# Cosine attention and a gated MLP on one core: filler products on TensorE, one more turn by DMA, another order

## The chip, the core and the metric

The kernel runs on one core of a Trainium2 chip. The core has five engines with queues of their own: TensorE (PE, matrix products, with a separate queue entry for each load of a stationary operand, PEld), VectorE (DVE), ScalarE (ACT), GpSimd (POOL) and SyncE (SP, which here only issues DMAs). PE writes to PSUM, which DVE and ACT read; POOL works on SBUF alone. Sixteen DMA engines carry all transfers.

The metric is the device time of one execution in microseconds (us). Runs of one kernel differ a little, so the median of several is given.

## The reference

Attention on normalised q and k, for 8 batches of 12 heads, 448 positions, 64 elements a head; its output, 3584 tokens of 768, goes through two products with a gate between them.

```python
q_n = q / (np.linalg.norm(q, axis=-1, keepdims=True) + 1e-06)
k_n = k / (np.linalg.norm(k, axis=-1, keepdims=True) + 1e-06)
scores = np.matmul(q_n, k_n.transpose(0, 1, 3, 2)) / tau
attn = softmax(scores)                      # written out in the reference
x = (attn @ v).transpose(0, 2, 1, 3).reshape(3584, 768)
h = x @ w_in                                # 768 x 2048
out = (h / (1 + np.exp(-1.702 * h))) @ w_out  # 2048 x 768
```

## The kernel before

**Tiling.** The work is cut into 24 groups of four heads, numbered y = 0 to 23, three to a batch. Inputs are fp32, products fp16 with fp32 sums. For each group: q and k are loaded (lines 260 to 276), squared on ACT, POOL or DVE (298), summed on DVE (307), and the reciprocal norms are made (323 to 376: on ACT and DVE for the first batch, by a Newton iteration on DVE later). `scale` (399) multiplies q and k by them into `qks`. Then the heads' positions must go from partitions to columns. There are two ways. For y < TURNED PE does it: `turn_qk` (424) is seven 128x128 products with the identity matrix into a PSUM tile, and `turned_qk` (434) copies that tile to `qkT` on DVE or ACT; this is done once for k and once for q. For the other groups `dma_turn` (442) issues two DMA transposes from `qks` to `qkT` on SP. `last_keys` (452) copies the last 64 keys into a matrix of their own.

Scores (461 to 497) go to tiles `sp`, of which there are two; ACT makes the exponentials (499 to 520); `attend` (522) multiplies them with v, eight products of 65 or 130 columns for each half, with a column of ones that gives the row sums; `normalise` (548) divides on DVE; the result `xs` is turned again, on PE (574, 583) or by DMA (609), to `xT`. The first batch is cut in two halves of the query positions so that its results come sooner.

The MLP follows: `mm1` or `mm1_h` (618, 647) with w_in, tanh on ACT (629), `gate` on DVE (635, 659), `mm2` (672) with w_out in parts of four products, `halve` (684) on ACT or DVE, and stores on SP. PSUM has four tiles `mm` for turns, attention and MLP, besides the two of `sp`.

**Order.** The kernel fixes the order of all instructions itself. A planner (class `Plan`, 61 to 183) holds every step with its engine, an estimated duration, a due time, the steps that it follows and the buffers that it takes and frees. `order` (102) plays them through in planned time: at each moment each engine takes, of its ready steps with free buffers, the one with the earliest due time. `emit` (85) then writes the instructions in that order; on each engine they run strictly in it. Due times are shifted by one character each of the string `DUES`; where a step may run on several engines, the string `ENGINES` chooses. Transfers are modelled by a rate per packet and a fixed latency `DMA_US`. PE's durations in the plan are of its full clock (seven turns 0.45 us, a half-attend pair 0.5).

Some loads are held back: w_in until v of y = 1 has landed, w_out until q of y = 5 has, and the loads of y = 6 and later until w_out has (`HOLD`, 730).

The lines that the change touches most:

```python
TURNED = 2 * ND                                        # line 717; ND is 3
if y < TURNED: ...                                     # 792: turns of q and k on PE, else dma_turn
turned = y < TURNED                                    # 841: turns of the attention output on PE
if y >= TURNED: ...                                    # 855: else dma_turn_x
```

Of the kernel before, what the change touches and what calls it, by code (L numbers as in the profile page):

```python
# [21 lines left out]
SWITCH_US = 0.093  # L22
DMA_US = 1.9
START_US = 0.74
DMA_ENGINES = 16
PACKET_US = {256: 0.033, 1024: 0.072, 1536: 0.064, 1792: 0.078, 3072: 0.135, 4096: 0.178}
MOE_FROM, MOE_LAG = 8, 9
STEPS = "#$%&()*+,-./0123456789:;<=>?@ABCDEFGHIJKLMNOPQRSTUVWXYZ[]^_abcdefghijklmnopqrst"
DUES = (
    "LKQtTEKJLtIKrKKQKKK#K?MC[YRQPIKPKKK:LC3KFMKWKXgB/VK7K;eC]KKIKLWAH@@KMEKFKTTKCLKKmFBCKHQK=P>RD4S5TlMK1VkI"  # L30
    "IEPLYK:U[K9VUPKJPNLK:tKKKJAKKgKSG?LJKKXWINKJOKkKGWXZXLrK9UKKLVKJKFM#K<qK[SVK#WFKDPOLLKctlKKJQIILeZHWJJ9Q"
    "bJKKKKM@KWKK5RKKLKIWH:IGh^BXKP?U5AJK1LFKtAJtc^UcKWKt@JM^MfKJdKeKKRMZKL9UK9qrMgGdrXKcALc__8iHLdtntKctNt@M"
    "qBMtEKeRtKtQYjj3[CVKMetIJSRKIKP0KOK<AY9Ns1PsTXWLJcHtRjO;[BKO*(J#KFPkLtKKhgrLKttKSKcSIKK?KKLKFtKKN0##KMPA"
    "tLK_LGKHXQCKKOG_[LT];KMISK<RMmK8KcAJ(=UKAPJgNLHqELEKZpKKIs<KaDKjfKdKWJ5K4LKKaLK2KILLJEJK;JKgKKKZRK=KESIJ"
    "#?XF[HLKK#RBgWCZMYWRKKIHK2K,S3,QPQ?OKFI8aQE<BG:M@?MHVUJPLKQEt>UZNSKJGi$B#EJRKR=LLLJF:JKG@OK_MUKZKEKS#G>W"
    "VK]H_J*+tU7OSKDMGhLGZKSV@IKI]DK4K3>KLSCt#Kb#KdKgtDIFIQNLJI&URUVlKKGNDULN&PTK#L>CPESGQOKKOJKKKRRDKKKsj330"
    "##KM8LOK^G0#YQWt>GI@KLKeKUOHGKKKEKMPK&BV#><d6feK(#KD5HRNKBQTXs:YgZKKK36Kb<?CTKjH5#P1%KIQCKBND>LXQOTaQKKQ"
    "IKWn/HKOSRQLKBKIS<KKNKMLRFJNFJKNXKXMDQ_j-AY#KJLKMK<KKEdKJ<KJKNWWMBJGIB8KKTVIQKK3D#3HH#7KKKAPJ,TB?WKCEIML"
    "KO$KKKMaK@KI;KKLNIU1/PBFZ$=mKMLS2KCK[GTK?G?KK;G#QKMMKAIKHKK8qWFLAF=6KEK=H8=:?KKNK.2KF27K<rMIMKKeKK;KKGKE"
    "EQA&BKKKKHK<K?#MFGQB?KD1&KK+KKJ$7IMfKJK^0QS*,QKjKROM(5DWRMWKXPQSKKIRTJ9Ab><D9CaBZ/0#SYKLKKJTIHK;PMKMLKJI"  # L40
    "+DL2:KFfAD7QKOGJJKOH1KFPPKEKSKTkF?G$P*<KdMKPMKRQKOKpKMCORKLI6MI(JU;LU#QLMKP5GKQKF)OGKLJNgN#[KKK^JJBM7DJ="
    "5KiKCOO9Li7NPPKMG_;UKKLIKIKIN*t=UHEF6S[K2JKKKKC-=O<LFKKJtKKJQNJQGIKhEH_KKKLQKCFJKRJKGKKTHtIKtKojtK9LKJO#"
    "JMCMJKTCHBotsCKT8@nQKRK#%KHpcBNKKk^oNKRJRI2FK:PN?KG=MKdIM<>FJNK^NKKLKEKGJKKLG?R/PEOYtKOBKJICSOqKp>QKDA6K"
    "OZ>#,YfKAIJXC@K#7FEJMPBKPOKJs3(K=KO_0LXGK(AKGOGOKO9=Fb:OK<F;:MMEVKKADA#CNLtLlK[ZXg3NU.KJTOUFQKQFPL#JLBKH"
    "EKJJti_KK?KKEKRRKW&X?RIOKOHKPK^RKILSKWOKAK@AKNKGHKKKIKVH=LJQK#OP=P1OKKZNLeVOLK#GSIKQU^AKQkrK(Bi>MKKKGPdb"
    "KIkstHttW"
)
ENGINES = (
    "02000101110101020101010101010001010101000201000101010001010101002100010101100101000101010001010201010100"
    "01010201010002000000010010220010020010100000101010101010101000100010211010100010100110101200101010101010"  # L50
    "101010101010101010001010101010101010101010101010"
)
# [8 lines left out]
class Plan:  # L61
# [22 lines left out]

    def emit(self, link):


        names, done, port = list(self.ops), {}, None
        for _, i, emit in self.order():
            eng, takes, hold = self.ops[names[i]][0], self.ops[names[i]][5], self.ops[names[i]][9]  # L90
            insts = emit(eng) if names[i] in self.alts else emit()
            insts = insts or (None,) if isinstance(insts, tuple) else (insts,)
            done[names[i]] = insts[-1]
            for h in hold:
                link(insts[0], done[h])
# [91 lines left out]
def kernel(  # L187
# [10 lines left out]
    nc = tc.nc  # L198
# [225 lines left out]
    def turn_qk(y, ti):  # L424
        ps = ps_m.tile([128, 512], FP32, name="mm").bitcast(FP16)[:, : 2 * S].rearrange("q (c s) -> q c s", c=C)
        for c in range(C):
            nc.tensor.transpose(  # L427
                out=ps[:, c],
                in_=qkss[y][:, ti, c].rearrange("p j d -> p (j d)"),
                identity=ident,  # L430
            )
        tpss[y, ti] = ps
# [19 lines left out]
    def last_keys(y, eng):  # L452
# [3 lines left out]
        )  # L456

    tpss, sps, avps, xss = [{} for _ in range(4)]
    rs_ps = ps_m.tile([128, 512], FP32, name="mm")[:, : ND * 4 * C].rearrange("p (y t j c) -> p y t j c", y=ND, t=2, j=2)
# [18 lines left out]
    def scores_h(y, g, h):  # L478
        if g < 2:
            sp = sps[y, g, h, "h"] = ps_s.tile([128, 2, 512], FP32, name="sp")  # L480
            for n in range(2):
                score(sp, y, g, n, SH * h, SH, SH * n)
        else:
            sp = sps[y, 2, h, "h"] = ps_s.tile([128, 2, 512], FP32, name="sp")
            for g in range(2):
                score(sp, y, g, 2, SH * h, SH, SH * g)

    def scores_l(y, h=None):
        sp = sps[y, "l", h] = ps_s.tile([128, 2, 512], FP32, name="sp")
        for g in range(2):  # L490
# [31 lines left out]
    def attend(x, h, short=False):  # L522
        ps = avps[x, h] = ps_m.tile([128, 512], FP32, name="mm")
        e, vt = exps[x // 2 % NE][:, x % 2], vts[x % NV]
        for i in range(2):
# [121 lines left out]
    def mm1_h(h, m):  # L647
        ps = mms[h, m, "h"] = ps_m.tile([128, 512], FP32, name="mm")
        for i in range(2):
# [66 lines left out]
    port = dict(takes=[("port", 1)], frees=[("port", 1)])  # L716
    TURNED = 2 * ND

# [19 lines left out]
    for y in range(NDUO):  # L738
# [22 lines left out]
        if first:  # L761
            for tis in ((1,), (0,)) if y == 0 else ((1, 0),):
                cut = slice(min(tis), max(tis) + 1)
                add(("root", tis[0], y), "ACT", 0.44, early + 0.2, partial(root, y, cut), after=[("red", ti, y) + (1,) * (y == 0) for ti in tis])
                add(("inv", tis[0], y), "DVE", 0.24 + 0.2 * len(tis), early + 0.2, partial(invert, y, cut), after=[("root", tis[0], y)],
                    frees=[(("n2", 1), int(0 in tis))])
                scales.update({ti: ("inv", tis[0], y) for ti in tis})
        else:
            if y == grp[0]:
                reds = [("red", ti, z) for z in grp for ti in range(2)]  # L770
                n = len(grp)
                add(("norm", 0, grp), "DVE", 0.7 + 0.1 * n, early + 0.3, partial(norm_a, grp), after=reds,
                    takes=[*port["takes"], (("nrm", n), 2 * n)], frees=port["frees"])
                add(("norm", 1, grp), "DVE", 1.1 + 0.3 * n, early + 0.3, partial(norm_b, grp), after=[("norm", 0, grp)],
                    takes=port["takes"], frees=[*port["frees"], (("n2", n), 1)])
            scales = {ti: ("norm", 1, grp) for ti in range(2)}
        for ti in (1, 0):
            dve = scale_on_dve(y, ti)
            add(("scale", ti, y), "DVE" if dve else "POOL", 1.1 if dve else 1.9, early + 0.5 if first else s - 5 - ti * 0.1,
                partial(scale, y, ti),  # L780
                after=[scales[ti]] + [("scale", 1, y)] * (not ti and y > 1), takes=[("qks", 2 if y < 2 else 4 * ti)],
                frees=[("qk", 1), (("nrm", len(grp)), int(not first))],
                alts=[("POOL", 1.9) if dve else ("DVE", 1.1)])
        for half in range(2):
# [45 lines left out]
        for g in range(2):  # L830
            x = 2 * y + g
            for h in range(2):
# [3 lines left out]
                else:  # L836
# [3 lines left out]
                    takes=[("mm", 1)], frees=[("exp", g * h), ("vt", h)])  # L840
                turned = y < TURNED
                whole = turned and not first
# [26 lines left out]
    for b in range(B):  # L869
# [3 lines left out]
        for u in units:  # L873
# [5 lines left out]
            elif m == 0:  # L879
                after += [("x", x, h) for x in range(b * HP, (b + 1) * HP) for h in range(2) if h and (x < 2 * TURNED or x % 2)]  # L880
            if b == 0:
# [81 lines left out]
    plan.tune(DUES, ENGINES)  # L963
    plan.emit(link)
# [33 lines left out]
```

## Time and profile before

| What | us |
|---|---|
| median of 11 runs | 440.24 (437.01 to 444.37) |
| the profiled execution | 443.84 |
| its span, first to last instruction | 441.9 |
| first product of PE | 7.71 |
| first MLP product | 37.87 |
| busy: PE, DVE, ACT, POOL | 412.7, 289.6, 260.0, 124.9 |

The profile is of one execution. A page gives the busy time of each engine, the span in 40 slices, the chain of work that ended last, and the costliest groups of instructions. Beyond the page, the trace was asked for a timeline (start, duration, engine, line and operation, output and inputs, shapes, and in brackets the idle time before and what ended it), for busy times by stretch, and for the chain of waits piece by piece. "mm<-ident,qks" is a product into tile mm with the identity and qks as operands.

The page's second part, 40 slices of 11.05 us each, in tenths of busy time:

```profile
PE   1697999978989899999999999999999999999996
ACT  4787788726865668676676557577752544413300
PEclk9999899989999999999999999999999999999999
DMA  8999398996787697998779878786433234011132
```

DMA is busy from the start and thins out after 300 us; PE has its gaps in the first dozen slices; ACT is busiest in the first third.

### The profile page before, as it was taken

Reading aid. Unit: us, or ns where it says so; the run is one execution under the profiler, and the core shown is the slowest. Engines: PE = TensorE matmul, PEld = TensorE weight load, DVE = VectorE, ACT = ScalarE, POOL = GpSimd, SP = SyncE. Lnnn points to the kernel's source line nnn. Section 1 sums busy time; section 2 is a strip of 40 time slices with the busy share of each in tenths; the row PEclk is TensorE's granted clock in tenths of the full one; section 3 lists DMA queues with packets and bytes.
Section 4 is the critical chain, followed back from the end, with each engine's and each line's share of the span. In section 5 each row is a group of like instructions: output and inputs, shape, how many; then the busy total and the mean of one; then the engine's idle time right before and its main releaser. Section 6 shows DMA issues by size and latency. Waiting matters only on the chain.

```text
span 441.9 us, 9229 instructions
## 1 busy us (share of the span) xinstructions
PE 412.7 (93%) x3614; PEld 247.0 (56%) x3614; DVE 289.6 (66%) x701; ACT 260.0 (59%) x383; POOL 124.9 (28%) x202
## 2 busy tenths in 40 slices
PE   1697999978989899999999999999999999999996
PEld 0366887644455555655554665555555555565563
DVE  6669898959997849875986858877842226424410
ACT  4787788726865668676676557577752544413300
POOL 4675261223323264433233343241320000000000
PEclk9999899989999999999999999999999999999999
DMA  8999398996787697998779878786433234011132
GB/s 267 241 222 264 81 182 195 271 213 175 147 189 185 158 212 172 194 155 213 155 172 203 177 188 176 160 163 82 64 64 72 55 74 79 1 43 29 32 76 71
DMA packets 84682, 64.88 MB, mean 147 GB/s; under 512 B 52768, under 2 KB 79648, under 8 KB 84640
## 3 DMA queue, kind: packets, MB, share of 16 engines
q1 hardware_dynamic: 80448, 57.36, 58.4%
q0 software_dynamic: 3744, 6.29, 7.9%
q8 instruction: 28, 0.46, 0.4%
q10 hardware_dynamic: 448, 0.66, 0.4%
q14 instruction: 14, 0.11, 0.1%
HBM read 47.19 MB, written 11.01 MB: 132 GB/s over the span
## 4 chain that ended last, share of the span: by engine, by line
PE 79%; DMA 7%; DVE 7%; SPq 2%; issue 2%; ACT 1%; POOL 1%; ACTq 0%; POOLq 0%; DVEq 0%
PE mm L621 28%; PE mm L676 28%; PE mm L539 8%; PE sp L465 7%; DMA qk<-in_q_dram 6%; PE mm L651 4%; PE mm L528 3%; DVE qks L404 2%; PE sp L491 2%; PE mm L427 1%; DMA qk<-in_k_dram 1%; SPq L282 1%; SPq L271 1%; DVE n L313 1%; ACT exp L500 1%
## 5 line engine op out<-in xcount | busy, mean ns | idle before, releaser
L500 ACT ACTIVATE exp<-sp 128x896 f16<-128x896 f32 (+1 forms) x171 | 147.2, 903 | 57.9 <-PE sp L465 50.7
L676 PE MATMUL mm<-w_out,gT 128*128 128x384 f16 x896 | 157.1, 328 | 1.1 <-DVE xs L567 1.1
L621 PE MATMUL mm<-xT,w_in 128*128 128x448 f16 x672 | 135.1, 353 | 1.9 <-DVE gT L638 1.5
L676 PEld LDWEIGHTS <-gT 128*128 128x128 f16 x896 | 84.7, 98 | 63.9 <-issue 9.4
L631 ACT ACTIVATE th<-mm 128x448 f16<-128x448 f32 x128 | 69.5, 545 | 65.4 <-PE mm L621 60.4
L621 PEld LDWEIGHTS <-w_in 128*128 128x128 f16 x672 | 63.4, 98 | 64.1 <-issue 8.0
L638 DVE SCALAR_TENSOR_TENSOR gT<-th,mm 128x448 f16<-128x448 f16 x112 | 67.8, 617 | 34.1 <-ACT th L631 30.9
L313 DVE TENSOR_REDUCE n<-sq 128x14 f32<-128x896 f32 (+1 forms) x50 | 51.7, 1043 | 13.2 <-ACT sq L305 11.1
L539 PE MATMUL mm<-vt,exp 128*128 128x65 f16 (+1 forms) x1152 | 58.3, 197 | 0.2 <-ACT exp L500 0.2
L539 PEld LDWEIGHTS <-exp 128*128 128x128 f16 (+1 forms) x1152 | 53.6, 102 | 6.6 <-issue 3.7
L528 PE MATMUL mm<-vt,exp 128*128 128x130 f16 x192 | 43.6, 227 | 4.2 <-ACT ost L690 2.7
L465 PE MATMUL sp<-qkT 64*128 64x448 f16 (+1 forms) x324 | 42.9, 349 | 4.3 <-ACT qkT L438 2.3
L689 DVE TENSOR_SCALAR ost<-mm 128x384 f32<-128x384 f32 x27 | 15.0, 554 | 43.8 <-PE mm L676 43.6
L567 DVE TENSOR_TENSOR xs<-mm,rc 112x256 f16<-112x256 f32 x96 | 40.8, 425 | 3.4
L551 DVE RECIPROCAL rc<-mm 112x4 f32<-112x4 f32 x96 | 17.0, 177 | 37.7 <-PE mm L539 37.4
L416 POOL CAST vt<-v 128x384 f16<-128x384 f32 x27 | 13.7, 506 | 86.5 <-PE mm L539 31.4
L305 ACT ACTIVATE sq<-qk 128x896 f32<-128x896 f32 (+1 forms) x30 | 27.3, 912 | 18.0 <-DMA qk<-in_q_dram 12.5
L404 POOL TENSOR_TENSOR qks<-qk,y 128x384 f16<-128x384 f32 (+1 forms) x36 | 25.7, 742 | 42.0 <-DVE y L372 21.7
L690 ACT ACTIVATE ost<-mm 128x384 f32<-128x384 f32 x29 | 14.2, 489 | 31.6 <-PE mm L676 28.6
L304 POOL TENSOR_TENSOR sq<-qk 128x896 f32<-128x896 f32 (+1 forms) x14 | 23.9, 1706 | 20.5 <-DVE kL L454 6.3
L405 POOL TENSOR_TENSOR qks<-qk,y 128x896 f16<-128x896 f32 x13 | 24.2, 1865 | 17.8 <-DVE vt L421 8.3
L528 PEld LDWEIGHTS <-exp 128*128 128x128 f16 x192 | 19.4, 101 | 11.4 <-issue 7.3
(59 smaller groups left out, 264.7 us busy)
## 6 DMA issues: line engine op xcount, KB each, us to landing
v<-in_v_dram SPq DMA_DIRECT2D x48, 256.0 KB, 5.5
out_dram<-ost SPq DMA_DIRECT2D x54, 192.0 KB, 3.0
qk<-in_k_dram SPq DMA_DIRECT2D x23, 448.0 KB, 5.0
qk<-in_q_dram SPq DMA_DIRECT2D x23, 448.0 KB, 4.2
w_in<-in_moe_w_in_dram POOLq DMA_DIRECT2D x8, 384.0 KB, 13.7
w_out<-in_moe_w_out_dram POOLq DMA_DIRECT2D x2, 1536.0 KB, 13.8
qkT<-qks SPq DMA_TRANSPOSE x36, 4.7
xT<-xs SPq DMA_TRANSPOSE x18, 3.1
```

The lines of the kernel that those rows point to most:

```text
L305: return nc.scalar.activation(out=dst, in_=src, func=AF.Square)
L313: return nc.vector.tensor_reduce(out=n2s[y][:, ti, js], in_=sqs[y, ti][:, js], axis=AX.X, op=ALU.add,)
L404: return tuple(eng.tensor_tensor(out=o, in0=a, in1=b, op=ALU.mult) for o, a, b in places(y))
L465: nc.tensor.matmul(out=sp[:, j, at : at + qn], lhsT=qkT[r, g, 1, 128 * n : 128 * (n + 1)], rhs=qkT[r, g, 0, q0 : q0 + qn], start=True, sto ...
L500: return nc.scalar.activation(out=dst, in_=src, func=AF.Exp, scale=inv_tau, **ekw)
L528: nc.tensor.matmul(out=o, lhsT=e[:, (C - 1) * S + a : (C - 1) * S + a + m], rhs=vt[:, 3].rearrange("p j d -> p (j d)"), start=True, stop=F ...
L539: nc.tensor.matmul(out=o[:, (D + 1) * j : (D + 1) * (j + 1)], lhsT=e[:, at : at + m], rhs=vt[:, n, j], start=False, stop=n == 2, skip_grou ...
L567: return nc.vector.tensor_tensor(out=xs, in0=ps[:, :, :D], in1=r[:, :, None].to_broadcast((P, 4, D)), op=ALU.mult,)
L621: nc.tensor.matmul(out=ps[:, :S], lhsT=w_in_sb[:, kk, 128 * m : 128 * (m + 1)], rhs=xTs[b, kk], start=(kk == 0), stop=(kk == KT1 - 1),)
L631: nc.scalar.activation(out=ths[key], in_=mms[key][:, :S], func=AF.Tanh, scale=0.851)
L638: nc.vector.scalar_tensor_tensor(out=gts[b // 2][:, m, (b % 2) * S : (b % 2 + 1) * S], in0=ths.pop((b, m)), scalar=1.0, in1=mms.pop((b, m) ...
L676: nc.tensor.matmul(out=mms[b2, t, n][:, :NW], lhsT=gts[b2][:, kk, 128 * t : 128 * (t + 1)], rhs=w_out_sb[:, kk, NW * n : NW * (n + 1)], st ...
```

## The change

It has four parts.

First, 64 products of the identity matrix with itself (128 columns) are issued on PE before everything else.

Second, filler products: while the plan's own time is under 48 us, `emit` measures the planned gap ahead of each PE step (its planned start less the planned end of the PE step before). The steps `turn_qk`, `scores_h`, `scores_l`, `attend` and `mm1_h` put (gap - 0.2) / 0.032 products of the identity with 64 of its columns ahead of their own, into unused or later overwritten columns of the PSUM tile that they have just taken. Nothing reads the fillers' results.

Third, `TURNED` goes from 6 to 5: q and k of y = 5 are turned by DMA. The turn of the attention output keeps its bound of 6 under the name `TX`.

Fourth, durations in the plan are longer for some steps (`DMA_US`, `inv`, `norm`, `scale`), and `DUES` and `ENGINES` are other strings, so all orders and many engines differ.

```diff
-DMA_US = 1.9
+DMA_US = 2.1
+FILL_TO, WARM_UP, FILL_US = 48, 64, 0.032
...
-    def emit(self, link):
+    def emit(self, link, gap):
-        names, done, port = list(self.ops), {}, None
-        for _, i, emit in self.order():
+        names, done, port, busy = list(self.ops), {}, None, None
+        for now, i, emit in self.order():
+            us = self.ops[names[i]][1]
+            if self.ops[names[i]][0] == "PE" and us:
+                if busy is not None and now < FILL_TO:
+                    gap(now - busy)
+                busy = now + us
...
     def turn_qk(y, ti):
-        ps = ps_m.tile([128, 512], FP32, name="mm").bitcast(FP16)[:, : 2 * S].rearrange("q (c s) -> q c s", c=C)
+        ps = ps_m.tile([128, 512], FP32, name="mm")
+        fill(ps[:, S:], 64)
+        ps = ps.bitcast(FP16)[:, : 2 * S].rearrange("q (c s) -> q c s", c=C)
...
+    gaps = []
+
+    def gap(us):
+        gaps[:] = [max(0.0, us - 0.2)]
+
+    def fill(corner, width):
+        n = int(sum(gaps) / FILL_US)
+        gaps.clear()
+        for _ in range(n):
+            nc.tensor.matmul(out=corner, lhsT=ident, rhs=ident[:, :width], start=True, stop=True, skip_group_check=True)
...
             sp = sps[y, g, h, "h"] = ps_s.tile([128, 2, 512], FP32, name="sp")
+            fill(sp[:, 1, S:], 64)
...
         ps = avps[x, h] = ps_m.tile([128, 512], FP32, name="mm")
+        fill(ps[:, 264:328], 64)
...
-    TURNED = 2 * ND
+    TURNED, TX = 5, 6
...
-                add(("inv", tis[0], y), "DVE", 0.24 + 0.2 * len(tis), early + 0.2, partial(invert, y, cut), after=[("root", tis[0], y)],
+                add(("inv", tis[0], y), "DVE", (0.45, 0.6)[len(tis) - 1], early + 0.2, partial(invert, y, cut), after=[("root", tis[0], y)],
...
-            add(("scale", ti, y), "DVE" if dve else "POOL", 1.1 if dve else 1.9, early + 0.5 if first else s - 5 - ti * 0.1,
+            add(("scale", ti, y), "DVE" if dve else "POOL", 1.2 if dve else 1.98, early + 0.5 if first else s - 5 - ti * 0.1,
...
-                turned = y < TURNED
+                turned = y < TX
...
-        if y >= TURNED:
+        if y >= TX:
...
-    plan.emit(link)
+    warm = ps_m.tile([128, 512], FP32, name="mm")
+    for _ in range(WARM_UP):
+        nc.tensor.matmul(out=warm[:, :128], lhsT=ident, rhs=ident, start=True, stop=True)
+    plan.emit(link, gap)
```

More of the change, by code (lines that the diff above doesn't have):

```diff
@@ L27 @@
 MOE_FROM, MOE_LAG = 8, 9
+FILL_TO, WARM_UP, FILL_US = 48, 64, 0.032
 STEPS = "#$%&()*+,-./0123456789:;<=>?@ABCDEFGHIJKLMNOPQRSTUVWXYZ[]^_abcdefghijklmnopqrst"
 DUES = (
-    "LKQtTEKJLtIKrKKQKKK#K?MC[YRQPIKPKKK:LC3KFMKWKXgB/VK7K;eC]KKIKLWAH@@KMEKFKTTKCLKKmFBCKHQK=P>RD4S5TlMK1VkI"
-    "IEPLYK:U[K9VUPKJPNLK:tKKKJAKKgKSG?LJKKXWINKJOKkKGWXZXLrK9UKKLVKJKFM#K<qK[SVK#WFKDPOLLKctlKKJQIILeZHWJJ9Q"
-    "bJKKKKM@KWKK5RKKLKIWH:IGh^BXKP?U5AJK1LFKtAJtc^UcKWKt@JM^MfKJdKeKKRMZKL9UK9qrMgGdrXKcALc__8iHLdtntKctNt@M"
@@ L33 @@
[L33 to L46, printed above, removed]
+    "tGmtOMKLKKMLTPUKXIKtBKATDQKOUH;K:LK#?K>L@]M8MKCE2e>MIKKbHg;BCJKFkIhKKTBLLUKRKrLMFJ]PAK;cgKYKHjpTqCKKXSNt"
+    "MKWgSFgKbtNiIT]C7K3KK5ZLtKGQKTcEGPKbFKJ/KtGetI7KAPKLLE?KCK#&@HNM%KMKKLEZk<JJW=KbTKKK@AEPKItMYKtWtETDsG9H"
@@ new lines @@
+    "fKSdCWssJLKRRK:KcGK[LHHGGXHt>JAKKcFtJBOOoNKPPMVa_MHN)ttsKTK@KLK@IKaKTiKKCOCInKoYKJKNHnLKRtCBKMLtth[tLtKK"
+    "WtttSsJtZPLRKJLHKLKNJKJIKDtKbM@ttQKfWLe@JtGMK;JtKt9KHRKKtKcSL#nsPPmiIqEptsYqKUtS=TMaG]1K1nLrs9[t(tLKeKn["
+    "NLSKKVK?KKKtHnf]#[@XMKLBJKc[ICt^3TQ-LN6JHL?<Ka#DtC)KKKIKO(SLPT+IKHSK>KKH#LCKU<KS@HKEI]?KW#GLKK?pLKWKmt3K"
+    "tKLK,IJKIKHFL(eGdJZKYRMEFQJCAPOtQM#K/hMKNdNNJ2LLEKPKKKNLKmJKN_T<KOs<t#GHODR?9LU;KOKMT2M9f4KN2#n*1sKT&LKK"
+    "Z3<KII3JKJPtKLIKGQStEG@cJsJ3tVKKKKEFtj9.MINAEKJH<KH@KQOE9KJIJ1JAGNHKGG:k$<K)OSBK#LKKRHFL?PLhKgKKfpX004;K"
@@ new lines @@
+    "6:tKhKkIK[tNHEKk8L1-KKSWPQI1B1@-L$FQ%dDK#Hp42K;NK(KJFI@&BKUXKKMPRMKG#0%##C1#_K-0JGZYhK#KLcNK8dfKM#J9HpKa"
+    "NGJ#Z54KKG)&-PJCF(@KGI7#KCNIG#MkLC<KJKJGV.10oKI7J#M[jM#9LJGIOKKbCMtKK]I]K8ESILPPKG#1&W%UK,JJHQU,+FMKKBJT"
+    "MH#K-YhRGd1KJHGEKMPKUGW_aMVKKO=er8JWRLNB@KKASG=Kf=AKUHp^KYHkX=QLJJRiJ>Kbs^UiKKKWIOK637KK$H=*KPKKMJKJP.4F"
+    "KD<RDKD6KK/KD3$J=AH*6G?=G4aF*.K:[KBLLJR+HH#OtHPJ@LLFME@8LVKIN#JKDS)N#UhKL#JNLK*HIBKO;KHt1HTDRKD2@UE7KKMK"
+    "MM&K9DIILC:?F?FK&:BWJ?HD]LbLK$5BCN/EY-L#QUMZJHMQ6KLMNJICGFEGO#BKNeohKTKVKGTBK3KLKLJ0ASONK7LL@OA3JKNVKKSO"
@@ L47 @@
+    "IRtNOKHOEIKJOXQHIENKJJtQO9K5S,MJSFTBORO@$QKE1DBLKI/HKKSFOKOKISHOKLJFgNDbHKKPNEKL[>PDLKBSDKnKK[2ZLKNTtKsQ"
+    "K]IEKVKY*KDKUKUNPJaOb_:SK7ZUMU=tOKHKK3#PJI;o_LK][MKLKKCI/HJa@K#;W+KK-tMXKKLtdG%KIqJEDTYRL,EhKJrKMQ5%HI[P"
+    "K#JMHWpNGDPSMINFB^ONJ_&K#K>#iaMj[RJMVLWKOEL_1KCHRTKKRPLFG*#KWPG%LICtI+@FKE9KKBPBK?K?W1=YFKKSMKQWK#?fIsMn"
+    "F[JF##KM.JK,4X#KPH)NDIQKQW67AK*KWFLV0EN5ORHM;KIJ/#PKBGQOJK0KPKHU[K+KFKKKQJMJ#Iec3b#KI;7LOH[KK6#KKD4OLBGK"
+    "ftKttL"
 )
 ENGINES = (
-    "02000101110101020101010101010001010101000201000101010001010101002100010101100101000101010001010201010100"
@@ L50 @@
-    "01010201010002000000010010220010020010100000101010101010101000100010211010100010100110101200101010101010"
-    "101010101010101010001010101010101010101010101010"
+    "00200100100101020000000011110010100000111020100110100001110101120000001112000002010000001010100110000211"
+    "10100010100101000000010000000100001000220000001000100000100220100000000000210111010001122101001000000010"
+    "0000100000010110100000100001100011000110100010"
 )
@@ L484, in scores_h @@
             sp = sps[y, 2, h, "h"] = ps_s.tile([128, 2, 512], FP32, name="sp")
+            fill(sp[:, 1, S:], 64)
             for g in range(2):
@@ L489, in scores_l @@
         sp = sps[y, "l", h] = ps_s.tile([128, 2, 512], FP32, name="sp")
+        fill(sp[:, 1, S:], 64)
         for g in range(2):
@@ L648, in mm1_h @@
         ps = mms[h, m, "h"] = ps_m.tile([128, 512], FP32, name="mm")
+        fill(ps[:, S:], 64)
         for i in range(2):
@@ L771 @@
                 n = len(grp)
-                add(("norm", 0, grp), "DVE", 0.7 + 0.1 * n, early + 0.3, partial(norm_a, grp), after=reds,
+                add(("norm", 0, grp), "DVE", 0.74 + 0.1 * n, early + 0.3, partial(norm_a, grp), after=reds,
                     takes=[*port["takes"], (("nrm", n), 2 * n)], frees=port["frees"])
-                add(("norm", 1, grp), "DVE", 1.1 + 0.3 * n, early + 0.3, partial(norm_b, grp), after=[("norm", 0, grp)],
+                add(("norm", 1, grp), "DVE", 1.13 + 0.3 * n, early + 0.3, partial(norm_b, grp), after=[("norm", 0, grp)],
                     takes=port["takes"], frees=[*port["frees"], (("n2", n), 1)])
@@ L782 @@
                 frees=[("qk", 1), (("nrm", len(grp)), int(not first))],
-                alts=[("POOL", 1.9) if dve else ("DVE", 1.1)])
+                alts=[("POOL", 1.98) if dve else ("DVE", 1.2)])
         for half in range(2):
@@ L879 @@
             elif m == 0:
-                after += [("x", x, h) for x in range(b * HP, (b + 1) * HP) for h in range(2) if h and (x < 2 * TURNED or x % 2)]
+                after += [("x", x, h) for x in range(b * HP, (b + 1) * HP) for h in range(2) if h and (x < 2 * TX or x % 2)]
             if b == 0:
```

## The prediction

> **What bounds the kernel now.** I read the page's first two parts first, then the busy time and clock by stage, then TensorE's timeline and the chain of waits for the first 100 us.
>
> ```profile
> PE 412.7 (93%) x3614; PEld 247.0 (56%) x3614; DVE 289.6 (66%) x701; ACT 260.0 (59%) x383; POOL 124.9 (28%) x202
> ...
> 148.00:438.00 290.00, 288.32 (x2369) 1.00 0.57 121
> ```
>
> TensorE (PE) is busy for 412.7 of 441.9 us, and from 148 to 438 us it idles for 1.7 us in all. So the end is set by how much work PE has to do and by what it loses before 148 us. The idle part of that loss: 7.7 us before the first product, 9.2 us between 9 and 44.3 us, about 8 us between 84 and 150 us. The other part is hidden in the busy time, as products that run at half speed:
>
> ```profile
> 20.54 0.56 PE L539 MATMUL mm<-vt,exp 128*128 128x65 f16 x6
> ...
> 27.73 0.93 PE L427 MATMUL mm<-ident,qks 128*128 128x128 f16 x7
> ...
> 44.37 0.35 PE L539 MATMUL mm<-vt,exp 128*128 128x65 f16 x6
> ...
> 56.99 0.56 PE L427 MATMUL mm<-ident,qks 128*128 128x128 f16 x7
> ```
>
> Same instruction, same shape: seven turns of q or k take 0.93 us at 27.7 and 0.56 at 57.0; six attention products 0.56 and 0.35. The change comes at 31.8 us; until then the array runs at half clock, although the clock column shows 1.00 there (its first record is that change; nothing is recorded before). Two later stretches are recorded:
>
> ```profile
> 42.00:45.42 3.42, 1.79 (x29) 1.00 1.09 252
> 45.42:48.83 3.41, 3.41 (x34) 0.50 0.68 159
> ...
> 89.79:93.20 3.41, 0.74 (x12) 1.00 1.08 270
> 93.20:96.62 3.42, 3.42 (x27) 0.50 1.21 160
> ```
>
> The columns are stretch, length, PE busy, granted clock, DMA share, GB/s. After 3.4 us in which PE was busy for only 1.79 or 0.74 us, the next 3.4 us run at half clock. A gap is thus paid twice.
>
> **Keeping the array warm.** The sum is made on the chain of waits. Before 18.3 us it runs over the loads of q and k (landed at 12.94), their squares and their scaling; a faster PE wins nothing there. From 18.3 to 31.3 us its PE pieces, cold, against the same pieces later in the same chain, warm: three sets of seven turns, 0.94 + 0.86 + 0.86 against 0.50 each, 1.16 saved; scores 0.56, 0.49, 0.88, 0.56, 0.49 against 0.32, 0.24, 0.49, 0.32, 0.24, 1.37 saved; eight half-attends 4.21 against 2.24, 1.97 saved; last-key scores and output turns, 0.47. Together 5.0 us. What is late next is ACT, which makes the exponentials: between 16.0 and 37.6 us it is busy for 17.6 of 21.6 us, so 4.0 us is all that goes before ACT is full with the work it has. The new engine string lightens it: read place by place, the turned q and k of the first twelve heads are copied by ACT once instead of four times (0.90 us each, 2.7 us less), which lifts that limit to 6.7. The first MoE weights do not forbid it: half of w_in's 3.1 MB has moved by 30 us, and the first MoE product starts at 37.9. Between 4.0 and 5.0 I take the nearer row, ACT's idle time: **-4.0 us**.
>
> A rule of the Trainium skill speaks against this. "TensorE: Matmul & The Clock Gate", in its part on the clock gate, says that about 3.4 us of sustained activity release the full clock, and that for modelling the ramp penalty is under 1% of a kernel. By that rule the array would be warm by about 12 us and only half of 3.4 us be lost: the gain would be at most 1.7 us. The trace decides otherwise: PE is busy for 3.30 of 3.41 us from 21.5 and still cold ten microseconds later.
>
> The second cold stretch, 45.4 to 48.8, is dense with work: at full clock it takes half, **-1.7 us**, if the stall before it (42.1 to 44.3, waiting for DVE's 4.2 us scaling) is filled or gone. The one at 93.2 lies past the 48 us at which filling ends: 0.
>
> **The fillers' own price.** The 64 warm-up products wait for the identity matrix (ready at 1.3 us); cold they take 64 x 0.107 (a cold set of seven turns is 0.75 apart in the chain) = 6.85, to 8.2 us. The first turn starts at 7.7: 0.5 us late at most, off the chain: 0. A 64-column filler goes by the row of 65-column attention products, six in 0.19 us warm, 0.032 each; cold six in 0.33, 0.055. The ten idle rows from 9 to 44.3 sum to 9.2 us; less 0.2 each that is 7.2 us, some 225 fillers, up to 430 if the 6.7 us that a warm PE frees are filled too. They cost nothing where PE waits for data. But a filler writes into the tile that the next product has just taken: where PE waited for that tile to be freed (25.5 and 37.6, by exp, 0.70 and 0.30), it starts after the wait and delays the product by as much again, less 0.2: +0.6. Cold throughout they would overrun by 225 x 0.023 = 5.2; below nothing they cannot go, their gain is counted above. I take **+0.6**, ends 0 and +5.
>
> **q and k of the sixth four heads by DMA.** Removed: 14 turns on PE and two copies.
>
> ```profile
> 73.30 0.55 PE L427 MATMUL mm<-ident,qks 128*128 128x128 f16 x7
> ...
> 87.69 7.77 SPq L445 DMA_TRANSPOSE qkT<-qks  x2
> ```
>
> PE is dense there (the other set starts at 70.92); from start to next start the two take 0.39 and 0.41: **-0.8 us**. The copies (0.61 DVE, 0.90 ACT) are hidden. Added: two DMA transposes on SP, median 1.70 us each, 3.4 us of queue, in a crowded stretch 7.8 (second row), landing 4.7 us after issue. The scores wait some 4 us longer for them; MoE products in PE's queue cover that. What stands behind them in SP's queue are the loads for the third batch, which go out from 73.1 to 81.7, and the last of these is waited for at 91.4. SP itself waits from 40.7 to 73.1 for w_out, so turns issued before that cost nothing; right ahead of the loads they cost 3.4. I take **+0.6**, ends 0 and +3.4 (below nothing it cannot go: the lighter DVE and ACT do not set the end there).
>
> The second rule against the change: "VectorE: DVE Perf Modes", rules for kernel authors, prefers TensorE for a 128x128 transpose, and gives 1309 ns by DMA against 390. By that, 14 blocks would cost 18.3 us instead of 5.5. The rows say 3.4 to 7.8 us of another queue against 0.8 of PE: whoever counts PE alone gains 0.8, whoever counts a full DMA loses up to 3.4.
>
> **The new order.** Every due time and many engines change: after the sixth four heads 13 us go from DVE to POOL (28% busy), and eleven output halvings from DVE to ACT. The larger DMA latency in the planner (2.1 for 1.9) bears on one stall that it misjudged:
>
> ```profile
> 88.95 0.95 ACT L305 ACTIVATE sq<-qk 128x896 f32<-128x896 f32 x1 [1.83 <-DMA qk<-in_k_dram]
> 91.49 0.95 ACT L305 ACTIVATE sq<-qk 128x896 f32<-128x896 f32 x1 [1.59 <-DMA qk<-in_q_dram]
> 92.35 0.47 ACT L690 ACTIVATE ost<-mm 128x384 f32<-128x384 f32 x1
> ...
> 92.87 0.22 PE L528 MATMUL mm<-vt,exp 128*128 128x130 f16 x1 [2.67 <-ACT ost L690]
> ```
>
> A halving that frees PE's output tile stands in ACT's queue behind two squares that wait for loads; PE stops for 2.67 us and runs cold after. Such stalls sum to 8 us with 1.7 of cold from 84 to 150 us. No row shows what another order makes of them: between -5 and +5, and more halvings on ACT speak for the second as the longer latency speaks for the first. I take 0.
>
> **Sum:** -4.0 - 1.7 + 0.6 - 0.8 + 0.6 = -5.3 us. The profiled execution took 443.84 us, 1.94 of it around the span; it becomes 438.5. The median of the runs shown is 440.24, 3.6 lower; I carry the same difference to it: **434.9 us**.
>
> **Rivals.** First, *the loads of the third batch set the pace*. PE arrives at the end of its work at 90.2 some 6.5 us sooner, finds the same load landing at 91.4, and gives back everything: 440.2. For it: DMA share above 1 from 76 to 96 us; w_out gates these loads. Against: w_out itself waits on POOL until 54.1 for a DVE chain, which an earlier start also moves, and PE has MoE work that needs no load.
>
> Second, on the other side, *the turn by DMA stands ahead of those loads on SP*. They go 3.4 us later, the landing moves from 91.4 to 94.8, the early gain is gone, and PE's longer gap makes one more 3.4 us stretch cold, 1.7: 440.2 + 3.4 + 1.7 - 0.8 = 444.5. It decides from the point where the turns are issued less than 3.4 us before the loads are free to go.
>
> Third, *the array does not warm*: gaps that the planner sees shorter than they are stay half empty, fillers run at 0.055 and overrun: 440.2 + 5.2 - 0.8 - 1.7 for the filled stall before 45 = 442.9.
>
> Fourth, the forecast and the stall at 90 gone with its cold stretch, 2.7 + 1.7: 430.5.
>
> **How the numbers follow.** Forecast 0.52 (431.5 to 438), its extension 0.11, load pace 0.15, turn ahead of loads 0.16, no warming 0.06. About 0.5%, 2.2 us, is what a measurement can tell from no change. Faster by more (under 438.0) 0.63, within 0.15, slower (over 442.4) 0.22. The range from 429.5 to 443.5 leaves out some 0.07 below and 0.12 above.
>
> **What would show it.** Right: seven turns in about 0.55 us from the second set of heads on; no half clock recorded between 20 and 50 us; the first MoE product near 33 to 34 us; PE instructions up by 64 - 14 and some 200 to 430; 38 DMA transposes of q and k, 70 turns. Wrong: ACT still idle for 4 us before 37 us, PE idle at 85 to 97 us growing by what was gained before, fillers right ahead of scores that ACT waits for, or new stalls past 100 us.

## The result, and the profile after

The changed kernel takes 436.7 us (median of 13 runs, 435.38 to 438.73) against 440.8 us for the kernel before (49 runs): ratio 0.991, 95% interval 0.9886 to 0.9935, some 4 us faster. Ratios leave out the executions that are more than 1.5% above the fastest of their kernel; the profiled execution of the kernel before, 443.84 us, on which the forecast rests, was one of these slow ones. Forecast were 434.9 us and -5.3 us. Direction and size were about right. The reason was not: the experiments below show that the part which the forecast counted on is worth nothing measurable, and that the part which it put at zero is enough for the whole gain.

The changed kernel also varies less: the middle half of its runs lies between 435.94 and 437.03 us, that of the kernel before between 439.15 and 442.27. What makes that spread was not tested.

The profiled execution of the changed kernel took 436.13 us. Its page, part 1 and two rows of part 2:

```profile
PE 415.3 (96%) x3893; PEld 254.1 (59%) x3893; DVE 265.1 (61%) x650; ACT 263.0 (61%) x393; POOL 139.9 (32%) x241
...
PE   6788999999999799999999999999999999999996
...
PEclk9999999999999899999999999999999999999999
```

PE has 279 instructions more: 64 warm-up products, 14 turns fewer, so 229 fillers (the forecast's count was 225). DVE lost 24.5 us of work, POOL gained 15, ACT 3. PE's timeline in the early stage of the same kernel:

```profile
10.38 1.80 PE L474 MATMUL mm<-ident 128*128 128x64 f16 x56
12.36 0.56 PE L434 MATMUL mm<-ident,qks 128*128 128x128 f16 x7 [0.19 <-POOL qks L410]
...
15.54 0.80 PE L474 MATMUL sp<-ident 128*128 128x64 f16 x22 [0.81 <-ACT exp L521]
...
36.42 1.31 PE L674 MATMUL mm<-xT,w_in 128*128 128x224 f16 x12
```

The array is warm: seven turns take 0.56 us at 12.4 us, where they took 0.93 in the prediction's row at 27.7. The third row shows fillers (ident, 64 columns) that begin only after a wait for ACT has ended. The first MLP product (the prediction calls the MLP "MoE") starts at 36.4 us, 1.5 us earlier than in the profiled execution of before and 0.2 us earlier than in a second one (36.65); the forecast said 33 to 34.

Busy time by stretch (length, PE busy, clock, DMA share, GB/s) shows the one cold stretch of the changed kernel between its first products and 430 us, and the dense part behind it:

```profile
145.46:148.87 3.41, 1.84 (x32) 1.00 0.86 194
148.87:152.28 3.41, 3.05 (x33) 0.50 0.72 196
152.28:430.00 277.72, 275.93 (x2224) 1.00 0.53 114
```

**Where the time went.** To compare two traces at any moment I count the products that PE has done, fillers aside, at the price that each kind has back to back and warm in the chain (448 columns of the MLP 0.189 us, 384 columns 0.1625, a score product of 448 columns 0.12, 65 columns 0.032, a turn 0.056, the few other kinds likewise), and call *lag* the time elapsed less that sum. It grows where PE idles, runs cold or runs fillers. "Before, second" is a further execution of the unchanged kernel (see the experiments).

| lag in us at | 40 | 50 | 90 | 110 | 140 | 165 | 225 | 400 |
|---|---|---|---|---|---|---|---|---|
| before (443.84) | 25.2 | 29.5 | 30.3 | 37.0 | 39.1 | 41.8 | 43.1 | 45.9 |
| before, second (438.53) | 24.1 | 28.1 | 29.4 | 31.6 | 34.7 | 36.6 | 37.8 | 40.6 |
| changed (436.13) | 24.1 | 25.9 | 26.8 | 28.0 | 28.8 | 34.6 | 36.6 | 39.4 |

Two things stand out. At 40 us the changed kernel is level with the second execution of before: whole kernel against whole kernel, nothing has been won by then. And the stall at 90 us (the first row jumps by 7 from 90 to 110) belongs largely to that one execution. Against the second row the changed kernel gains 2.2 us from 40 to 50, 3.3 between 90 and 140, and gives 4.7 back between 140 and 225, where PE waits 2.3 us for exponentials (146 to 150), runs cold after it, and stops for 1.06 and 0.73 us later. At 400 us it is 1.2 us ahead of the second trace and 6.5 ahead of the first; the medians, 4 us apart, lie between. Two traces show where such differences arise, not how large each is in the median.

### The profile page after: what moved, and what is told of

It is laid out like the page before. It is cut to its first block, busy times and chain, and to the rows that moved or that the text cites. A ratio compares the mean times of both kernels' runs of the same rounds, so it can differ in the third digit from the quotient of the medians.

```text
span 434.3 us, 9761 instructions
## 1 busy us (share of the span) xinstructions
PE 415.3 (96%) x3893; PEld 254.1 (59%) x3893; DVE 265.1 (61%) x650; ACT 263.0 (61%) x393; POOL 139.9 (32%) x241
## 4 chain that ended last, share of the span: by engine, by line
PE 79%; DMA 10%; DVE 4%; POOL 2%; ACT 2%; issue 1%; SPq 0%; ACTq 0%; POOLq 0%
PE mm L699 32%; PE mm L643 26%; PE mm L561 7%; PE sp L483 6%; DMA qk<-in_q_dram 4%; PE mm L674 4%; PE mm L550 2%; DMA qk<-in_k_dram 2%; DMA w_in<-in_moe_w_in_dram 2%; DMA v<-in_v_dram 2%; PE sp L512 2%; DVE n L318 2%; POOL qks L409 1%; ACT exp L521 1%; DVE gT L660 1%
## 5 line engine op out<-in xcount | busy, mean ns | idle before, releaser
L699 PEld LDWEIGHTS <-gT 128*128 128x128 f16 x896 | 83.8, 98 | 61.8 <-issue 8.9
L561 PE MATMUL mm<-vt,exp 128*128 128x65 f16 (+1 forms) x1152 | 56.5, 195 | 0.0
L561 PEld LDWEIGHTS <-exp 128*128 128x128 f16 (+1 forms) x1152 | 51.9, 100 | 5.2 <-issue 2.3
L421 POOL CAST vt<-v 128x384 f16<-128x384 f32 x34 | 18.7, 550 | 103.1 <-PE mm L561 54.9
L713 ACT ACTIVATE ost<-mm 128x384 f32<-128x384 f32 x40 | 19.7, 492 | 50.0 <-PE mm L699 46.0
L483 PE MATMUL sp<-qkT 64*128 64x448 f16 (+1 forms) x324 | 41.2, 335 | 2.7 <-ACT exp L521 2.3
L573 DVE RECIPROCAL rc<-mm 112x4 f32<-112x4 f32 x96 | 17.1, 178 | 39.6 <-PE mm L561 39.4
L409 POOL TENSOR_TENSOR qks<-qk,y 128x384 f16<-128x384 f32 (+1 forms) x45 | 30.6, 707 | 29.5 <-DVE y L377 11.7
L309 POOL TENSOR_TENSOR sq<-qk 128x896 f32<-128x896 f32 (+1 forms) x16 | 26.2, 1635 | 24.8 <-DMA qk<-in_q_dram 9.4
L712 DVE TENSOR_SCALAR ost<-mm 128x384 f32<-128x384 f32 x16 | 8.9, 556 | 38.5 <-PE mm L699 38.5
L410 POOL TENSOR_TENSOR qks<-qk,y 128x896 f16<-128x896 f32 x13 | 22.3, 1712 | 7.5 <-DVE kL L461 6.8
```

Source lines behind the costliest of these rows:

```text
L409: return tuple(eng.tensor_tensor(out=o, in0=a, in1=b, op=ALU.mult) for o, a, b in places(y))
L483: nc.tensor.matmul(out=sp[:, j, at : at + qn], lhsT=qkT[r, g, 1, 128 * n : 128 * (n + 1)], rhs=qkT[r, g, 0, q0 : q0 + qn], start=True, sto ...
L561: nc.tensor.matmul(out=o[:, (D + 1) * j : (D + 1) * (j + 1)], lhsT=e[:, at : at + m], rhs=vt[:, n, j], start=False, stop=n == 2, skip_grou ...
L699: nc.tensor.matmul(out=mms[b2, t, n][:, :NW], lhsT=gts[b2][:, kk, 128 * t : 128 * (t + 1)], rhs=w_out_sb[:, kk, NW * n : NW * (n + 1)], st ...
```

## The experiments

Two theories: **the warm clock** (the forecast) and **the new order**. Each run has its own runs of the kernel before on the same chip; ratios are to those.

**1. Parts of the change taken away.** Order alone:

```diff
-FILL_TO, WARM_UP, FILL_US = 48, 64, 0.032
+FILL_TO, WARM_UP, FILL_US = 0, 0, 0.032
```

> The changed kernel without its 64 warm-up products and without fillers (no part of the result is left out): new order and the turn by DMA alone. If the warm clock is the gain, as forecast (4.0 + 1.7 - 0.6), all of it is lost and the time is 441 to 442.5 us, with the array cold until past 25 us. If the gain is the new order (second stretch of loads earlier, no stall at 90 us), it stays within 1 us of 436.7. A share of each, as the comparison of the two traces suggests (3.6 us up to 50 us, the rest later): 439 to 440.5.

Measured: 436.41 us, ratio 0.9916 (0.9885 to 0.9947). All of the gain is there without one filler. (The trace is of the slowest of its 12 executions, 439.63 us, with stops of 1.59 and 0.71 us at 267 and 278 us that the trace of the changed kernel does not have; what follows is read ahead of 150 us.) The array was cold for long, as this clock shows (busy by stretch):

```profile
16.00:25.40 9.40, 8.53 (x80) 1.00 1.13 253
...
25.40:28.81 3.41, 1.84 (x22) 1.00 1.13 210
28.81:35.64 6.83, 6.45 (x68) 0.50 1.12 231
```

(Before 25.4 us no clock is recorded; its seven turns take 0.93 us there.) And between 95 and 140 us PE does not stop at all:

```profile
95.00:140.00 45.00, 45.00 (x385) 1.00 0.86 193
```

In this order the fillers do bring PE forward. Without them the first MLP product comes at 38.96 us, with them at 36.42:

```profile
38.96 1.31 PE L674 MATMUL mm<-xT,w_in 128*128 128x224 f16 x12
```

The gain shrinks from there. With fillers PE stops for 1.23 us at 40.4 and 1.08 at 45.2, both times for DVE; without them one such stop is left there, of 0.75. The lag without fillers is 26.9 us at 50, 1.0 more than with them. At 110 us the two are level (27.8 and 28.0), in part because the kernel with fillers, arriving sooner, waits 0.5 us for DVE at 100 us. What is gained early is waited away.

Warm-up without fillers (`FILL_TO = 0, WARM_UP = 64`):

> The changed kernel with the 64 warm-up products but no fillers. If the gaps between 7 and 20 us are long enough to send the array back to half clock, this is no better than without both: 440 to 442 us, and the granted clock shows 0.50 in at least one stretch before 25 us. If one warm-up is enough, 436.5 to 437.5 and no such stretch.

Measured: 436.03 us, ratio 0.9913 (0.9881 to 0.9945). The clock was full from 4.6 us and fell back at 11.4 for 13.7 us, as the first case said; the time is that of the second. So neither case holds as a whole: the clock in this stage does not reach the end.

No fillers ahead of the scores (the three `fill(sp[:, 1, S:], 64)` taken out):

> The changed kernel without the fillers ahead of the scores (ten groups, about 155 of 229 products); those ahead of turns and attention products stay. By the forecast's price they delay the scores by 0.6 us in all: 436.1. If they hold ACT back, which idles 1.9 us at 18.5 and some 0.5 us three times after: 434.5 to 435.5. If they are what keeps the clock up: 438 to 440, with half clock recorded before 35 us.

Measured: 436.76 us, ratio 0.9939 (0.9915 to 0.9963). The array fell to half clock three times before 45 us, as the third case said, but the time is that of neither the second nor the third. No gain and no loss that can be told from the changed kernel: the price of +0.6 us is as invisible as the gain.

**2. Fillers in the old order**, turns on PE: warm-up, `gap`, `fill` and its calls put into the kernel before.

> The kernel before with warm-up and fillers alone, order and turns as they were. Forecast: 440.8 - 4.0 - 1.7 + 0.6 = 435.7 us. If PE only reaches the loads of the third batch sooner and waits there (first rival): 439.5 to 441, with PE idle between 84 and 97 us grown by 2 us or more. If the fillers overrun: 442 or more.

Measured: 442.45 us, ratio 1.0049 (1.0014 to 1.0084): slower, and the time of the third case. Its trace does not show the overrun of that case: the first MLP product comes at 37.5 us, between the two traces of before (37.9 and 36.65). The stall ahead of 100 us is 2.1 us, but it is the same stall, for a halving on ACT, that the prediction read at 2.67, and two stops of 1.7 us together with a cold stretch come at 293 us, waiting for exponentials. Which of these makes the median 2 us longer stays open; one trace does not settle it. That the fillers give no gain alone is shown.

**3. The loads of w_out.** They gate the third batch's loads; the new order issues them at 49.8 instead of 54.1 and 57.1 us. In the old order both loads, ("w_out", 0) and ("w_out", 1), are moved ahead of one POOL step; nothing else moves:

```diff
+    def moved(self, names):
...
+        w = [out[first], out[last]]
+        rest = [o for o in out if o not in w]
+        return rest[:ahead] + w + rest[ahead:]
...
-        for _, i, emit in self.order():
+        for _, i, emit in self.moved(names):
```

> The kernel before (no fillers, turns on PE) with one move: both loads of w_out are issued on POOL ahead of the one v cast that waits there until 53 us, so they go out when q of y = 5 has landed, near 49.5 us instead of 54.1 and 57.1. Nothing else changes its place. If the loads of the third batch, which wait for w_out, set the stall at 90 us and this is what the new order gained: those loads go out near 69 us instead of 73, the stall of 2.7 us and its cold stretch are gone, and the time is 435.5 to 437.5. If the gain of the new order lies elsewhere (work moved from DVE to POOL, other places): 439.5 to 441.

Measured: 439.79 us, ratio 0.9978 (0.9954 to 1.0002). The loads went out at 49.8 and the third batch's at 68.7, as expected. Of the stall at 89 us 0.7 us was left; the second trace of before has 0.26 without the move, so that this trace does not show what the move did to it. The gain is about 1 us by the medians' ratio, and the interval goes from none to 2.

This trace shows something else, by chance. Up to 49 us PE has the same order as in the second trace of before, and the same stop of 1.24 us for the scaling on DVE (first two rows: second trace, this run). Yet the clock fell in the one and not in the other (third and fourth row):

```profile
42.56 0.23 PE L427 MATMUL mm<-ident,qks 128*128 128x128 f16 x1 [1.24 <-DVE qks L404]
41.57 0.23 PE L436 MATMUL mm<-ident,qks 128*128 128x128 f16 x1 [1.24 <-DVE qks L413]
...
43.04:46.45 3.41, 3.36 (x43) 0.50 1.10 279
41.45:44.87 3.42, 2.94 (x50) 1.00 1.07 298
```

So the lead of the warm run over the cold one grew from 1.0 us at that stop to 2.1 at 47.5 us, where 24 MLP products start (49.63 us in the cold one). But the turns of the next q and k, again in the second trace and then in this run, read:

```profile
55.60 0.56 PE L427 MATMUL mm<-ident,qks 128*128 128x128 f16 x7
...
55.22 0.59 PE L436 MATMUL mm<-ident,qks 128*128 128x128 f16 x6 [1.44 <-POOL qks L413]
```

The warm PE came 1.4 us early to a scaling on POOL that was done at the same time as in the cold trace (55.5 and 55.7 us), and waited; behind these turns its lead is 0.35 us (55.65 against 56.00). A warm stretch was won without any filler, and 8 us later nothing of it was left.

The reverse move in the changed kernel, two and four POOL steps later:

> The changed kernel with the reverse move: the two loads of w_out go two and four POOL steps later, near 55 and 58 us instead of 49.8 and 50.7. If the start of w_out is what the order gained, this gives it back: 439.5 to 441, with the third batch's loads near 75 us and a stall of PE between 88 and 100. If not: 436.5 to 437.5.

Measured: 443.5 us, ratio 1.0067 (1.0038 to 1.0096), worse than either case. PE's timeline says why:

```profile
76.49 1.44 PE L708 MATMUL mm<-w_out,gT 128*128 128x384 f16 x4 [4.50 <-DMA w_out<-in_moe_w_out_dram]
```

PE waited for w_out itself, 4.5 us, and ran at half clock for 6.8 us, from 74.7 to 81.5. The third batch's loads were not what stopped it. An early w_out is something the new order needs; that it is what the order gained, this run does not show.

**4. The turn by DMA.** Back on PE in the changed kernel:

```diff
     def dma_turn(y):
+        if y == 5:
+            turn_qk(y, 1)
+            k = turned_qk(y, 1, "DVE")
+            turn_qk(y, 0)
+            return k, turned_qk(y, 0, "ACT")
```

> The changed kernel with q and k of y = 5 turned on PE again, at the same place of the order (14 products, two copies on DVE and ACT, no DMA transposes for them). Forecast: the turn by DMA saved 0.8 us of PE, and its two transposes stand on SP at 63 us, while SP waits, at no cost: 437.5. If a copy more in the queues of DVE and ACT, or an mm tile more, delays others: 438.5 or more. If the transposes cost DMA time that the loads miss: 435.5 to 436.5.

Measured: 437.33 us, ratio 0.9923 (0.9894 to 0.9952) against 0.991 (0.9886 to 0.9935). That agrees with 0.6 us for the turn by DMA, and with none: too small to be told here.

By DMA in the old order, where the second copy had stood (SP's order otherwise unchanged):

> The kernel before with q and k of y = 5 turned by DMA where the second of the two copies stood, so that on SP the two transposes come behind the loads of q and k of y = 6 and ahead of all later ones; last keys on POOL. The second rival: the loads behind go out 3.4 us later and PE, whose order is not changed, waits for the turned heads: 444 to 446. If the loads have that much room: 440 to 441.

Measured: 444.54 us, ratio 1.0085 (1.0057 to 1.0113), 3.4 us over the kernel before by the medians: the time of the second rival. The place of the loss, in PE's timeline:

```profile
77.29 0.93 PE L475 MATMUL sp<-qkT 64*128 64x448 f16 x4 [4.11 <-DMA qkT<-qks]
```

PE waited 4.1 us for the turned heads, with a cold stretch from 77.2 to 80.6; that puts its lag at 34.4 us at 90, 5 over the second execution of before. It is the wait that I had called covered by MLP products, and it is covered only if the order puts such products there. In the changed kernel the transposes are issued at 63.2 us and the scores wait for nothing.

**5. DVE.** With the loads accounted for, what was left was the stretch from 95 to 145 us. First, less work on DVE at unchanged places, with w_out early:

```diff
+RELIEF = {
+    ('scale', 0, 6): 'POOL',
...
+    ('ost', 0, 1, 0): 'ACT',
...
+            eng = RELIEF.get(names[i], eng)
```

In all 11 steps go to POOL and 5 halvings of the output to ACT.

> The kernel before with w_out early (as in the run of that name) and, at unchanged places, 16 steps of groups 6 to 11 and of the first MLP pair taken off DVE as the new engine string has them: six v casts, three scalings and two last-keys steps to POOL, five output halvings to ACT, some 12 us of DVE between 85 and 165 us, where DVE is 85 to 95% busy. If a full DVE is what still stops PE there (5 us of lag from 95 to 140 us against 1.4 in the changed kernel): 436.5 to 438. If the order of the steps is what does it: 439 to 441, like w_out early alone.

Measured: 439.67 us, ratio 1.0015 (0.9984 to 1.0047): nothing. DVE is busy for 35.5 us between 95 and 140 us, where it was 40.6 with w_out early alone. PE's stops:

```profile
89.73 1.46 PE L705 MATMUL mm<-w_out,gT 128*128 128x384 f16 x8 [1.01 <-ACT ost L719]
...
105.74 5.83 PE L650 MATMUL mm<-xT,w_in 128*128 128x448 f16 x30 [1.56 <-DVE gT L667]
```

The largest stop for DVE is as long as it was, and PE now also waits for halvings that were moved to ACT (1.01 us here, 0.53 at 100.2). The stops for divisions on DVE, 1.1 and 0.9 us with w_out early alone, are gone. So less work on DVE and more on ACT bring nothing together; what less work on DVE would bring alone was not tested.

Second trace of the kernel before:

> The kernel before, unchanged, for a second trace. If the stall of 2.7 us at 90 us with its cold stretch is typical, it shows again; if it belonged to that one execution (443.84, 3 us over its median), this one is near 440 and has less of it.

One execution, 438.53 us; the stall at 89 us is 0.26 us. So the 2.7 us that the prediction quoted are not the kernel's usual stall; with fillers in the old order it was 2.1, with w_out early 0.7. The stops behind it are the same in both (in the first trace at 108.5 and 126.1 us):

```profile
103.12 5.83 PE L621 MATMUL mm<-xT,w_in 128*128 128x448 f16 x30 [1.51 <-DVE gT L638]
...
120.49 0.82 PE L676 MATMUL mm<-w_out,gT 128*128 128x384 f16 x4 [1.11 <-DVE xs L567]
```

and DVE's timeline at the first of them:

```profile
99.81 2.72 DVE L404 TENSOR_TENSOR qks<-qk,y 128x384 f16<-128x384 f32 x3
102.45 1.67 DVE L638 SCALAR_TENSOR_TENSOR gT<-th,mm 128x448 f16<-128x448 f16 x3
```

A scaling of 2.7 us, for scores that are not due for long, stands ahead of three gates (merged into one row); each gate frees one of PE's output tiles. PE runs out of tiles and stops. The last experiment turns just that round: in the kernel before, on DVE alone, between 80 and 150 us of planned time, a sum, scaling, cast or last-keys copy goes behind the one to three gates or divisions that stood right behind it, if nothing in between needs it.

```diff
+            if 80 < now < 150 and self.ops[name][0] == "DVE" and name[0] in ("scale", "red", "cast", "kL", "sq") and name not in self.late:
...
+                    if other[0] not in ("g", "nx") or out[r][0] > end + 0.1 or past == 3:
+                        break
+                    to, past, end = r, past + 1, out[r][0] + self.ops[other][1]
```

> The kernel before with nothing changed but DVE's own queue between 85 and 150 us: about ten sums, scalings and casts go behind the one to three gates or divisions that stood right behind them; the other four engines keep their orders. In the second trace of the kernel before, PE stops in that stretch for 0.4, 1.5, 1.1 and 1.2 us, each time until DVE has done a gate or a division that stood behind such a step, and by 140 us it lags 5.9 us behind the changed kernel. If that place in DVE's queue is what the new order gained: at least half of these 4.2 us, 436.5 to 438. If engines and loads are only shifted into another wait: 439.5 to 441.

Measured: 437.8 us, ratio 0.9948 (0.9919 to 0.9976): 2.3 us by the medians, over half of the change's gain (the interval goes from a quarter of it to nearly all), from the order of about ten steps on one engine. DVE's timeline and PE's there:

```profile
100.86 0.62 DVE L668 SCALAR_TENSOR_TENSOR gT<-th,mm 128x448 f16<-128x448 f16 x1 [0.92 <-ACT th L661]
101.39 1.45 DVE L434 TENSOR_TENSOR qks<-qk,y 128x384 f16<-128x384 f32 x3
...
103.43 4.70 PE L651 MATMUL mm<-xT,w_in 128*128 128x448 f16 x24 [0.53 <-DVE gT L668]
```

A gate now runs ahead of the scaling. The stop of 1.5 us is 0.5, those of 1.1 and 1.2 us are 0.3 and 0.2; the lag from 100 to 150 us grows by 4.4 instead of 6.5. The trace has no half clock near 45 us either, but that is not the gain: at 90 us its lag is level with that of the second trace.

**6. A version beyond both?** The changed kernel with warm-up, no fillers, and w_out one POOL step earlier still:

> The changed kernel with its 64 warm-up products, without fillers, and with both loads of w_out one POOL step earlier still (ahead of a scaling that waits for DVE until 47.8 us). DMA stands idle from 48 to 52 us. If the loads still pace PE: 435 to 435.8, better than the changed kernel. If PE is no longer held by them: 436 to 436.7.

Measured: 436.4 us, ratio 0.9925 (0.9897 to 0.9953). w_out went out at 47.7 us, and a scaling behind it came late (PE stopped 1.4 us at 52). That is the second case: no better. No version here beats the changed kernel by more than can be told.

## Why the prediction was right in time and wrong in cause

The sum came out near the measured time because two terms were wrong and made up for each other: -5.1 us was counted for fillers that bring nothing that can be measured, and nothing for an order that is enough for the whole gain. That is luck.

**What bounds the kernel**: right. PE's total and what it loses before 150 us set the end; in the changed kernel PE is busy for 275.9 of the 277.7 us from 152 us on.

**Keeping the array warm, -4.0 us**: the step that failed. Most of its facts held: the array was cold to 31.8 us, it is warm from 5.5 us on now, and the cold pieces shrink (seven turns from 0.93 to 0.56 us). But a sum of shortened pieces along a chain is not a gain at the end; it is the most that could be gained if nothing else waited. I named ACT as the next limit and took its 4.0 us of idle time for the gain. In the changed kernel ACT is busy for 17.4 of the same 21.6 us: it still idles 4.2, which the prediction had named as a sign of being wrong. PE in turn waits there for ACT (fillers fill such waits; they do not end them), and at 40 us the lag is that of the second execution of before, 24.1 us. Against the same order without fillers PE is ahead by 2.5 us at the first MLP product and level at 110 us. The runs without fillers give the same time as with them.

The rule of the Trainium skill that I set aside, "TensorE: Matmul & The Clock Gate" in its part on the clock gate, puts the ramp penalty under 1% of a kernel. One per cent is 4.4 us here, so that the forecast's 4.0 did not break it; the estimate of at most 1.7 us that I drew from the same part would have been nearer: the order alone measures 436.41 us against 436.7 with all fillers. For its other half, that some 3.4 us of activity release the clock, the trace was rightly preferred: it was cold to 31.8 us. (That the rule has the array warm by about 12 us was my reading; PE idles for 2.95 us just ahead of 11.94, so its activity there was not sustained.) It did not matter.

**The second cold stretch, -1.7 us**: the mechanism is real (a stretch of 3.4 us in which PE is half busy, then 3.4 us at half clock, again in the second trace from 43.0 us) and it is gone. But it is gone without fillers too: from 35.6 us the order alone stays at full clock until 148. Nor is it clear that the order removed it. It comes and goes between executions: in the old order the run with w_out early and the last DVE run have none, in the new order the run without fillers ahead of the scores has one (41.0 to 44.4 us). And where it is missing in the old order, PE is level again at 90 us. The 1.7 us is a real length and not a gain at the end.

**Fillers +0.6**: not visible in the new order (436.76 us without those ahead of the scores); in the old order the whole of fillers and warm-up costs 0.5%.

**Turn by DMA, -0.8 + 0.6**: agrees with the run, which cannot tell it from zero. The second rival priced the bad place of the transposes at 444.5 us, and the bad place measured 444.54. The loads behind them did go out some 3.5 us later (v at 76.2 us, in the second trace of before at 72.6). But half of its mechanism was wrong: PE waited for the turned heads, not for those loads. And the rival's sum is of 4.3 us over 440.2, the run is 3.4 over its own kernel before; that both end at 444.5 is chance.

**The new order, 0**: the term that was mis-sized. Alone, with the turn, it measures -3.9 us (436.41 against 440.31). In the old order the place of ten DVE steps is worth 2.3 us and an early w_out about 1 (0 to 2); the turn by DMA is worth some 0.6 in the new one and cannot be told from nothing. That these are the parts of the 3.9 us, and that they add up, is argued from the sizes, not shown. The prediction looked at the largest stall of one trace (2.7 us at 90 us) and priced no other singly. It was the largest stall that shrank to 0.26 us in a second trace, and the smaller ones that came back.

**The first rival** (the third batch's loads set the pace, and an early gain is given back there): w_out early sent these loads out 3 to 4 us sooner and gained about 1 us, so they are not the pace. Its form was right, its place was not: the early gain is given back, at waits for POOL and DVE between 40 and 100 us. **The third** (no warming) did not happen.

## What to carry to other kernels

Before counting what a faster engine gains, find what it will wait for at the end of the stage: a chain's shortened pieces are an upper bound. When engines work off strict queues, read what stands ahead of the steps that free the bottleneck's buffers; long steps with time to spare belong behind them, and moving work to another engine without changing places may bring nothing. Take a stall, or a cold stretch, for typical only when a second trace shows it.

## What the runs showed of the hardware

In these traces the clock changes only at steps of 3.41 us or multiples of it (31.76, 45.42, 48.83, 93.20 and 96.62 us in the first trace of before). Counted in such steps, PE's busy time draws no sharp line. After 1.79 us (42.00 to 45.42, the kernel before), 1.84 (145.46 to 148.87, the changed one) and 1.57 (39.63 to 43.04, second trace of before) the next step ran at half clock. After 1.90 (106.86 to 110.27, the kernel before) and 1.95 (38.04 to 41.45, w_out early) it did not. The last and the 1.57 are the same stop of 1.24 us in the same order; it lies within one step in the one trace and across the end of a step in the other, which may be why the clock fell in one alone.

In the other direction busy time does not decide alone either. Counting the steps back from the first record, PE was busy for 3.41 of 3.41 us from 19.15 in the second trace of before, and seven turns still took 0.93 us at 24.86; 3.26 of 3.41 us released the clock at 25.4 in the run of the order alone. And a group of 22 fillers in the changed kernel broke off after the first for 1.30 us at 17.9 us with nothing that the profile shows to wait for; no run here tells what that was.
